# One of four sets of a group's first dense product by seven block products, in a fused attention and MLP kernel

## The chip, the cores and the metric

The kernel runs on one core of a Trainium2 chip. The metric is the device time of one execution in microseconds. The engines are TensorE (PE, with PEld for weight loads), VectorE (DVE), ScalarE (ACT), GpSimd (POOL) and SyncE (SP), which here issues nearly all DMA.

## The reference

Four batches, eight heads, 768 positions, head size 64. For each head, attention with decay `lam` runs over blocks of 64 positions with a carried state; its result is a matrix `x` of 3072 tokens by 512 features. Then comes a dense layer pair:

```
intra = (qb @ kb.T * Dmask) @ vb
inter = (qb * lam_pow) @ kv_state
kv_state = lam**64 * kv_state + (kb * rev_pow).T @ vb
x = (intra + inter), heads side by side          # 3072 x 512
h = x @ w_in                                     # 512 -> 2048
g = gelu_tanh(h)
out = g @ w_out                                  # 2048 -> 512
```

q, k, v and the output are float32; the products inside are in float16 with float32 accumulation.

## The kernel before, in words

**Attention.** There are 24 steps: 12 blocks of 256 tokens, each in two halves of four heads. For a step `s`:

- `load_step` brings q, k and v of the step into pools of four buffers each (`q32`, `k32`, `v32`).
- `cast_qk` (L278, L283) scales q on VectorE and casts k on ScalarE. `scale_v` (L266) scales v on GpSimd. `prep_v` is `scale_v` and the request for the loads of three steps later.
- `transpose_dma` (L293) lays q and k out transposed, by a DMA, in the pool `qkp`. `prep_qk` is `cast_qk` and `transpose_dma`.
- `burst(ns, ss)` does a pair of steps at once: scores S of the steps `ns` (L340), products O of the probabilities of the steps `ss` with v (L424), products K of k and v of the steps `ns` (L438), products of the state u with q of the steps `ss` (L449). VectorE masks the scores into PT (L350) and updates the state t (L491, L494), GpSimd writes u from t (L501), and ScalarE takes the attention result out of PSUM into `xT` (L475).

**The dense layers.** The 12 blocks form seven groups, `[[0, 1], [2], [3], [4, 5], [6, 7], [8, 9], [10, 11]]`, numbered from 0; a group of two blocks has 512 tokens. When a group's `xT` is complete, `queue_group` puts the pieces of its dense products into a list, `filler`. `fill(n)` runs the next n pieces. The calls of `fill` between the parts of the attention are written by hand, so that TensorE has dense work while VectorE, ScalarE and GpSimd prepare the next step.

- First product, plain: `mm1` (L542) makes 128 rows of h for 512 tokens by four products of 128 x 512, and ScalarE's gelu (L546) writes them into `gT`. A group of two blocks has 16 such pieces.
- First product, by seven: for groups in `SEVEN = (5, 6)` (the sixth and seventh) h is cut into four sets. In a set, the blocks of h (two halves of f by two halves of the tokens, contracted over two halves of c) are made from seven block products instead of eight, after Winograd's form of Strassen's scheme. `seven(m, k)` (L711) is product m of set k: four products of 128 x 256. Sums of `w_in` (`sum_win`, L151) and of `xT` (`sum_x`, L690) are the operands. Intermediate results are added outside of TensorE: copies by ScalarE and VectorE (L722, L724), additions by VectorE (L732). PSUM banks HX, HW and HY are opened by products 1, 2 and 5. HX takes products 1, 6, 7 and 4 in turn, and each next product waits until the result so far has been copied or added.
- Second product by seven for the groups from the second on: `product` (L619) with `sum_g` (L589) on VectorE.

[...] a new tile takes a bank whose last reader is done. The order on each engine is the order in which the program is written.

**Around the change.** The fifth group (number 4: blocks 6 and 7, steps 12 to 15) is queued when step 15 is done, in `R(17, 15)`, near 105 us. Its first product runs from 112.65 us, before, between and after the bursts of the steps 18 and 19, and 20 and 21. VectorE makes the last sums of `w_in` (`sum_win(3, ...)`, `sum_win(4, ...)`) just before, since the sixth group needs them.

The lines that bear on it:

```
SEVEN = (5, 6)
...
for i in range(HF):
    for fs in ([[i, i + HF]] if per == 2 else [[i], [i + HF]]):
        filler.append(lambda fs=fs: mm1(fs))
...
            if k == HF // 2 - 1 and m in (3, 7, 4):
                release()
```

`release` issues the gelus that are held back in `pending`; in a set other than the last they wait for product 5 of the next set.

Of the kernel before, what the change touches and what calls it, by code (L numbers as in the profile page):

```python
# [8 lines left out]
FP32 = mybir.dt.float32  # L9
# [6 lines left out]
def kernel(  # L16
# [12 lines left out]
    P = 128  # L29
# [12 lines left out]
    const = ctx.enter_context(tc.tile_pool(name="const", bufs=1))  # L42
# [1 line left out]
    wst = ctx.enter_context(tc.tile_pool(name="wst", bufs=1))  # L44
    ld = ctx.enter_context(tc.tile_pool(name="ld", bufs=4))
    a16p = ctx.enter_context(tc.tile_pool(name="a16", bufs=5))
    qkp = ctx.enter_context(tc.tile_pool(name="qkp", bufs=4))
    ptp = ctx.enter_context(tc.tile_pool(name="ptp", bufs=3))
    ucp = ctx.enter_context(tc.tile_pool(name="ucp", bufs=3))
    ubp = ctx.enter_context(tc.tile_pool(name="ubp", bufs=4))  # L50
# [3 lines left out]
    otp = ctx.enter_context(tc.tile_pool(name="otp", bufs=3))  # L54
# [23 lines left out]
    HF, HE = NF // 2, DM // 2  # L78
# [91 lines left out]
    def load_ahead(s):  # L170
        if s < NSTEP:
            load_step(s)
# [13 lines left out]
                   allow_small_or_imprecise_dtypes=True)  # L186
    nc.gpsimd.tensor_scalar(pos[64:128], pos[64:128], 128.0, None, ALU.subtract)

    rel = const.tile([P, 2, 2, 64], FP32)
    nc.gpsimd.iota(rel[:], pattern=[[-1, 2], [1, 2], [2, 64]], base=0, channel_multiplier=-2,  # L190
                   allow_small_or_imprecise_dtypes=True)
    ident = const.tile([P, P], FP16)
# [30 lines left out]
    def odd(hs):  # L223
        pin(nc.vector.tensor_tensor(dq[:, hs, 1], dq[:, hs, 0], lam_bc[:, hs], ALU.mult))

    def inverse(hs):
        pin(nc.vector.reciprocal(dv[:, hs], dq[:, hs]))
# [21 lines left out]
    def wide(t):  # L249
        return t.rearrange("p j h d -> p h j d")  # L250

    def decay(t, s):
        hs = halves[s % 2]
        return t[:, hs, :].unsqueeze(3).to_broadcast([P, HH, 2, D])

    def prep_v(s):
        scale_v(s)
        if s >= 6:
            if s + 3 == FIRST_DMA_T + 1:
                load_step(s + 3, "qk")  # L260
            else:
                load_ahead(s + 3)

    def scale_v(s):
        tv = a16p.tile([P, 2, HH, D], FP16, tag="v16", name=f"v16_{s}")
        pin(nc.gpsimd.tensor_tensor(wide(tv[:]), ld32[s][2][:], decay(dv, s), ALU.mult))  # L266
        a16[s] = a16[s] + (tv,)

    def prep_qk(s):
        cast_qk(s)  # L270
        transpose_dma(s)

    def cast_qk(s):
        q32, k32, _ = ld32[s]
        tqk = a16p.tile([P, 2, 2, HH, D], FP16, tag="qk16", name=f"qk16_{s}")
        tq, tk = tqk[:, 0], tqk[:, 1]
        q_eng = nc.gpsimd if s == 3 else nc.vector
        pin(q_eng.tensor_tensor(wide(tq), q32[:], decay(dq, s), ALU.mult))  # L278
        if s == 0:
            inverse(halves[0])  # L280
            odd(halves[1])
            inverse(halves[1])
        pin(nc.scalar.activation(out=wide(tk), in_=k32[:], func=AF.Copy))  # L283
        a16[s] = (tq, tk)
        whole_qk[s] = tqk
# [3 lines left out]
    def transpose_dma(s):  # L289
        tqk = whole_qk.pop(s)  # L290
        if s >= FIRST_DMA_T:
            o = qkp.tile([P, 2, 2, 2, P], FP16, tag="qkT", name=f"qkT_{s}")
            pin(nc.sync.dma_start_transpose(out=o[:].rearrange("p a j h t -> p (a j h) t"),  # L293
                                            in_=tqk[:].rearrange("p a j h d -> p (a j h d)")))
            qkT[s] = o
            if s == FIRST_DMA_T:
                load_step(s + 1, "v")
# [219 lines left out]
        return gs_kept[1:]  # L517

    SEVEN = (5, 6)
    SLOTS = {5: {1: 0, 2: 1, 5: 1, 6: 1, 3: 1, 7: 1}, 4: {1: 0, 2: 1, 5: 0, 6: 1, 3: 1, 7: 1}}  # L520
    groups = [[0, 1], [2], [3], [4, 5], [6, 7], [8, 9], [10, 11]]
    group_of = {sb: (g, i) for g, sbs in enumerate(groups) for i, sb in enumerate(sbs)}
    filler = []

    def queue_group(g, lead=0, per_set=0):
# [168 lines left out]
        def release():  # L694
            while pending:
                pending.pop(0)()

        def seven(m, k):

            st = of_set.setdefault(k, {})  # L700
            for name in {1: "X", 2: "W", 5: "Y"}.get(m, ""):
                key = name + str(k % 2) if name == "X" else name
                if key not in hbank:
                    hbank[key] = ps_M.tile([P, 2, SB], FP32, tag="M", name="H" + name)
                st[name] = hbank[key]
            dst = st[{2: "W", 5: "Y", 3: "Y"}.get(m, "X")]
            a, b = X_FACTORS[m]
            for i in range(2):
                f = 2 * k + i
                for c in range(2):  # L710
                    pin(nc.tensor.matmul(  # L711
                        dst[:, i, :],
                        w_in_block(a, slice(c, c + 1), slice(f * P, f * P + P))[:, 0],
                        x_block(b, slice(c, c + 1))[:, 0],
                        start=(m in (1, 2, 5) and c == 0 and i == 0), stop=(m in (2, 3, 4) and c == 1),
                        skip_group_check=True))

            def copied(name, tag, eng):
                t = ld.tile([P, HH, 2, D], FP32, tag=tag, name=f"{name}_{g}_{k}")
                t = t[:].rearrange("p h j d -> p (h j d)").rearrange("p (i t) -> p i t", i=2)  # L720
                if eng is nc.scalar:
                    pin(nc.scalar.activation(out=t, in_=dst[:], func=AF.Copy))  # L722
                else:
                    pin(eng.tensor_copy(out=t, in_=dst[:]))  # L724
                st[name] = t

            def gelu(F, T, src):
                pin(nc.scalar.activation(out=gT[:, 2 * k : 2 * k + 2, F, T * SB : T * SB + SB],
                                         in_=src, func=AF.Gelu_apprx_tanh))

            def added(F, T, name):
                pin(nc.vector.tensor_tensor(st[name], dst[:], st[name], ALU.add))  # L732
                pending.append(lambda src=st[name]: gelu(F, T, src))

            if m == 1:
                copied("m1", "q32", nc.scalar)
            elif m == 2:
                added(0, 0, "m1")
            elif m == 5:
                copied("q", "q32", nc.scalar)  # L740
                release()
            elif m == 6:
                copied("u2", "k32", nc.vector)
            elif m == 3:
                added(0, 1, "u2")
            elif m == 7:
                added(1, 1, "q")
            elif m == 4:
                pending.insert(0, lambda: gelu(1, 0, dst[:]))
            if k == HF // 2 - 1 and m in (3, 7, 4):  # L750
                release()

        def merge(lead, per_set):
# [22 lines left out]
            unread = {1: 16, 2: 12, 4: 8, 3: 4}  # L776
            slots = SLOTS[per_set]
            for k in range(HF // 2):
# [46 lines left out]
        def behind(k, i0, i1, ms):  # L825

            piece = filler[at + k]

            def both():
                piece()  # L830
                sum_g(i0, i1, ms)

            filler[at + k] = both

        at = len(filler)
        order = [(m, p) for m in (1, 2, 5, 6, 3, 7, 4) for p in range(HN // P)]
        if g in SEVEN:
            merge(lead, per_set)
            parts = (0, 1) if g + 1 in SEVEN else (None,)
            for m, p in order:  # L840
# [3 lines left out]
            for k, m in enumerate((2, 4, 3)):  # L844
                behind(len(parts) * k, 4, 8, (m,))
            return
        for i in range(HF):
            for fs in ([[i, i + HF]] if per == 2 else [[i], [i + HF]]):
                filler.append(lambda fs=fs: mm1(fs))
        for m, p in order:  # L850
            for part in (0, 1) if g + 1 in SEVEN else (None,):
                filler.append(lambda m=m, p=p, part=part: product(m, p, part))

        n1 = HF * (2 // per)
        if per == 2:
            behind(5, 0, 4, (1, 2))
            behind(6, 0, 4, (4, 3))
            behind(7, 4, 8, (1,))
            behind(8, 4, 8, (2,))
            behind(9, 4, 8, (4,))  # L860
            behind(10, 4, 8, (3,))
        else:
            behind(9, 0, 4, (1, 2) if g == 3 else (1, 2, 4, 3))
            if g == 3:
                behind(12, 0, 4, (4, 3))
            w = 2 if g + 1 in SEVEN else 1
            for k, m in zip((0, 3, 7, 11) if w == 2 else (0, 1, 2, 4), (1, 2, 4, 3)):
                behind(n1 + k, 4, 8, (m,))

    def fill(n):  # L870
        for _ in range(min(n, len(filler))):
            filler.pop(0)()
# [17 lines left out]
    def U(n):  # L890
        update(n, 1)
# [118 lines left out]
        if n > 8:  # L1010
            sum_win((n - 7) // 2, (n - 1) % 2, nc.vector)

    cast_qk(16)
    scale_v(16)
    fill(3)
    burst((13, 14), (12,))
    transpose_dma(16)
    fill(1)
    U(13)
    U(14)  # L1020
    load_ahead(18)
    load_ahead(19)
    fill(2)
    cast_qk(17)
    scale_v(17)
    fill(3)
    burst((15, 16), (13, 14))
    transpose_dma(17)
    load_ahead(20)
    fill(1)  # L1030
    U(15)
# [12 lines left out]
    sum_win(4, 0, nc.vector)  # L1044
    fill(2)
    sum_win(4, 1, nc.vector)
    fill(2)
    prep_qk(20)
    fill(1)
    prep_qk(21)  # L1050
    prep_v(20)
    fill(3)

    burst((18, 19), (16, 17))
    prep_v(21)
    fill(2)
    U(18)
    U(19)
    fill(4)
    prep_qk(22)  # L1060
    fill(2)
    burst((20, 21), (18, 19), 11, 4)
# [43 lines left out]
```

## Time and profile before

| what | value |
|---|---|
| median of 3 runs | 199.54 us (199.5 to 199.82) |
| span of the profiled execution | 197.7 us |
| TensorE busy | 191.4 us, 97% |
| VectorE, ScalarE, GpSimd busy | 154.0, 122.8, 75.1 us |
| TensorE clock granted | 1.0 over the whole span |
| plain first product of the fifth group | 20 products from 112.81, 32 from 118.95, 12 from 127.49 us |

The span is counted from the first to the last instruction of the profiled execution; the median time is some 1.8 us above it. The page gives for each group of instructions the line, engine and operation, the tiles written and read, count, busy time and mean duration, and the idle time of the engine before it with what ended it.

### The profile page before, as it was taken

How to read it: one execution, taken by the hardware profiler on the slowest of the kernel's cores; microseconds unless marked ns; L12 is line 12 of the kernel's file. 1: busy time of each engine (PE TensorE's matmuls, PEld its weight loads, DVE VectorE, ACT ScalarE, POOL GpSimd, SP SyncE). 2: the span in 40 equal slices, each digit the busy share in tenths (PEclk: the TensorE clock that was granted, in tenths of full speed). 3: DMA queues.
4: the chain of work that ended last, by engine and by line, in shares of the span. 5: the costliest groups of instructions: out<-in, count | busy, mean ns of one | idle time of the engine just before them, and what ended most of it. 6: DMA issues, size and time to landing. Idle time of an engine off the chain costs nothing.

```text
span 197.7 us, 5935 instructions
## 1 busy us (share of the span) xinstructions
PE 191.4 (97%) x2439; PEld 139.8 (71%) x2439; DVE 154.0 (78%) x296; ACT 122.8 (62%) x251; POOL 75.1 (38%) x85
## 2 busy tenths in 40 slices
PE   8879999999999999999999999999999999999993
PEld 2546544456888888754588854578888888888882
DVE  4987722789999989969999927998778996588620
ACT  3673878467794675677645377854768836778221
POOL 6594223456557652455563526156002030002000
PEclk9999999999999999999999999999999999999999
DMA  6999999999999999999993998620211200030205
GB/s 168 290 324 386 386 385 389 297 285 310 335 259 265 218 308 226 195 274 179 286 221 74 235 326 101 174 56 0 53 59 51 106 9 0 0 109 1 106 4 212
DMA packets 61722, 37.86 MB, mean 192 GB/s; under 512 B 17536, under 2 KB 54656, under 8 KB 61696
## 3 DMA queue, kind: packets, MB, share of 16 engines
q1 hardware_dynamic: 61152, 37.23, 74.1%
q8 instruction: 19, 0.31, 0.7%
q10 hardware_dynamic: 544, 0.26, 0.5%
q14 instruction: 7, 0.06, 0.1%
HBM read 27.26 MB, written 6.29 MB: 170 GB/s over the span
## 4 chain that ended last, share of the span: by engine, by line
PE 88%; SPq 4%; DMA 4%; ACT 1%; issue 1%
PE Hps L542 24%; PE MX L619 17%; PE MY L619 9%; PE HX L711 7%; PE O2ps L557 7%; PE MW L619 4%; DMA wi<-in_moe_w_in_dram 4%; SPq L70 4%; PE HY L711 4%; PE S L340 3%; PE Hps L802 3%; PE HW L711 2%; PE OK L398 2%; PE O L449 1%; PE O L424 1%; PE Tps L311 1%
## 5 line engine op out<-in xcount | busy, mean ns | idle before, releaser
L542 PE MATMUL Hps<-xT,w_in 128*128 128x512 f16 (+1 forms) x288 | 50.8, 332 | 0.0
L501 POOL TENSOR_TENSOR u<-t,lumask 128x256 f16<-128x256 f32 x40 | 31.0, 790 | 46.2 <-DVE t L494 28.3
L542 PEld LDWEIGHTS <-w_in 128*128 128x128 f16 x288 | 27.8, 98 | 19.1
L546 ACT ACTIVATE gT<-Hps 128x512 f16<-128x512 f32 x56 | 33.1, 598 | 9.3 <-PE Hps L542 8.8
L350 DVE TENSOR_TENSOR PT<-S,mask 128x512 f16<-128x512 f32 x48 | 30.3, 681 | 6.3 <-PE S L340 6.3
L619 PEld LDWEIGHTS <-gs 128*128 128x128 f16 x320 | 31.2, 98 | 3.6
L266 POOL TENSOR_TENSOR v<-v,dv 128x512 f16<-128x512 f32 x24 | 29.6, 1236 | 8.0 <-DMA v<-in_v_dram 7.7
L619 PEld LDWEIGHTS <-gT 128*128 128x128 f16 x240 | 23.2, 98 | 3.6 <-ACT gT L546 0.5
L619 PE MATMUL MX<-w_sum,gs 128*128 128x256 f16 x160 | 21.4, 273 | 0.0
L278 DVE TENSOR_TENSOR qk<-q,dq 128x512 f16<-128x512 f32 x23 | 19.8, 863 | 0.7 <-DMA q<-in_q_dram 0.7
L664 POOL TENSOR_TENSOR o<-u,q 128x512 f32<-128x512 f32 (+1 forms) x5 | 5.8, 1159 | 37.7 <-ACT u L636 37.7
L283 ACT ACTIVATE qk<-k 128x512 f16<-128x512 f32 x24 | 15.0, 625 | 6.6 <-DMA k<-in_k_dram 6.5
L589 DVE TENSOR_TENSOR gs<-gT 128x1024 f16<-128x1024 f16 (+1 forms) x24 | 17.6, 737 | 1.5 <-ACT gT L546 1.5
L557 PE MATMUL O2ps<-w_out,gT 128*128 128x512 f16 x64 | 14.6, 379 | 0.0
L475 ACT ACTIVATE xT<-OK 128x256 f16<-128x256 f32 x26 | 10.0, 455 | 7.3 <-PE OK L398 7.2
L711 PEld LDWEIGHTS <-ws 128*128 128x128 f16 x128 | 12.5, 97 | 1.8
L636 ACT ACTIVATE u<-MX 128x256 f32<-128x256 f32 x18 | 6.9, 384 | 10.2 <-PE MX L619 10.2
L475 ACT ACTIVATE xT<-O 128x256 f16<-128x256 f32 x22 | 8.0, 460 | 5.9 <-PE O L449 5.0
L557 PEld LDWEIGHTS <-gT 128*128 128x128 f16 x64 | 6.1, 98 | 6.6
L619 PE MATMUL MY<-w_out,gs 128*128 128x256 f16 x80 | 10.7, 273 | 0.0
L340 PEld LDWEIGHTS <-qkT 64*64 64x64 f16 x384 | 6.0, 106 | 6.5 <-issue 3.0
L589 DVE TENSOR_TENSOR gs<-gs,gT 128x1024 f16<-128x1024 f16 (+1 forms) x12 | 10.2, 852 | 0.3
(95 smaller groups left out, 318.7 us busy)
## 6 DMA issues: line engine op xcount, KB each, us to landing
q<-in_q_dram SPq DMA_DIRECT2D x24, 256.0 KB, 5.0
k<-in_k_dram SPq DMA_DIRECT2D x24, 256.0 KB, 5.3
v<-in_v_dram SPq DMA_DIRECT2D x23, 256.0 KB, 5.4
out_dram<-o SPq DMA_DIRECT2D x19, 256.0 KB, 4.0
wo<-in_moe_w_out_dram SPq DMA_DIRECT2D x4, 1024.0 KB, 9.5
wi<-in_moe_w_in_dram SPq DMA_DIRECT2D x4, 512.0 KB, 8.1
wi<-in_moe_w_in_dram SPq DMA_DIRECT2D x2, 1024.0 KB, 12.8
out_dram<-o SPq DMA_DIRECT2D x2, 512.0 KB, 6.8
```

The lines of the kernel that those rows point to most:

```text
L266: pin(nc.gpsimd.tensor_tensor(wide(tv[:]), ld32[s][2][:], decay(dv, s), ALU.mult))
L278: pin(q_eng.tensor_tensor(wide(tq), q32[:], decay(dq, s), ALU.mult))
L283: pin(nc.scalar.activation(out=wide(tk), in_=k32[:], func=AF.Copy))
L350: pin(nc.vector.tensor_tensor(t[:, hl].rearrange("p b c d -> p b (c d)"), Sps[:].rearrange("p b c d -> p b (c d)"), mask[:].unsqueeze(1).t ...
L475: pin(nc.scalar.activation(out=d, in_=o, func=AF.Copy))
L501: pin(nc.gpsimd.tensor_tensor(u[:], state[half][:].unsqueeze(2).to_broadcast([P, 2, 2, D]), lumask[:, 2 * half : 2 * half + 2, :].unsqueez ...
L542: pin(nc.tensor.matmul(by_block(Hps[:, i, :]), w_in16[:, c, f * P : (f + 1) * P], x(c), start=(c == 0), stop=(c == NC - 1)))
L546: pin(nc.scalar.activation(out=dst, in_=Hps[:], func=AF.Gelu_apprx_tanh))
L557: pin(nc.tensor.matmul(O2[tau][0][:], gT[:, f % HF, f // HF, tau * P : (tau + 1) * P], w_out16[:, f, :], start=(n == 0), stop=(n == NF - 1)))
L589: pin(nc.vector.tensor_tensor(g_rows(m, i), g_rows(a, i), g_rows(b, i), op))
L619: pin(nc.tensor.matmul(dst, lhsT, rhs, start=(opens and i == 0), stop=(closes and i == HF - 1), skip_group_check=True))
L711: pin(nc.tensor.matmul(dst[:, i, :], w_in_block(a, slice(c, c + 1), slice(f * P, f * P + P))[:, 0], x_block(b, slice(c, c + 1))[:, 0], sta ...
```

## The change

One of the four sets of the fifth group's first product (f = 0, 1, 8, 9) is made by seven block products; the other twelve pieces stay plain. The pieces of the set are queued alternating with three of the plain ones, and the gelus are issued as soon as their operands are there. The sums of `w_in` exist already at that time, the sums of `xT` (`sum_xs[0](m)`) are called by hand. To go with it, the pool `qkp` gets a fifth buffer, and `rel`, which is needed only at the start, takes a buffer of the pool of outputs to make space. Transposes of steps 16 and 17 are issued with their casts, and the hand-written order around the bursts of steps 18 to 21 moves: all the seven products of the set come ahead of the burst of 18 and 19, and v of steps 20 and 21 is scaled later.

```diff
-    qkp = ctx.enter_context(tc.tile_pool(name="qkp", bufs=4))
+    qkp = ctx.enter_context(tc.tile_pool(name="qkp", bufs=5))
...
-    rel = const.tile([P, 2, 2, 64], FP32)
+    rel = otp.tile([P, 2, 2, 64], FP32, tag="o32", name="rel")
...
+    MIXED = 4
+    sum_xs = []
...
-            if k == HF // 2 - 1 and m in (3, 7, 4):
+            if (k == HF // 2 - 1 or g == MIXED) and m in (3, 7, 4):
                 release()
...
-        for i in range(HF):
+        if g == MIXED:
+            sum_xs.append(sum_x)
+            plain = [[f] for i in range(2, HF) for f in (i, i + HF)]
+            for m in (1, 2, 5, 0, 6, 3, 0, 7, 0, 4):
+                filler.append((lambda m=m: seven(m, 0)) if m else (lambda fs=plain.pop(0): mm1(fs)))
+            for fs in plain:
+                filler.append(lambda fs=fs: mm1(fs))
+        for i in range(HF) if g != MIXED else ():
...
-            behind(9, 0, 4, (1, 2) if g == 3 else (1, 2, 4, 3))
+            n1 += 3 * (g == MIXED)
+            behind(n1 - 7, 0, 4, (1, 2) if g == 3 else (1, 2, 4, 3))
...
-    cast_qk(16)
+    prep_qk(16)
     scale_v(16)
     fill(3)
     burst((13, 14), (12,))
-    transpose_dma(16)
     fill(1)
...
-    cast_qk(17)
+    prep_qk(17)
     scale_v(17)
     fill(3)
     burst((15, 16), (13, 14))
-    transpose_dma(17)
     load_ahead(20)
...
     sum_win(4, 1, nc.vector)
-    fill(2)
+    for m in (1, 2, 3, 4):
+        sum_xs[0](m)
     prep_qk(20)
-    fill(1)
+    fill(3)
     prep_qk(21)
+    fill(8)
+
+    burst((18, 19), (16, 17))
     prep_v(20)
-    fill(3)
-
-    burst((18, 19), (16, 17))
-    prep_v(21)
     fill(2)
     U(18)
     U(19)
-    fill(4)
+    prep_v(21)
+    fill(2)
     prep_qk(22)
     fill(2)
     burst((20, 21), (18, 19), 11, 4)
```

## The prediction

> **What bounds the kernel now.** I read the page's busy times and slices first, then the chain of waits, then the table of stretches around the change, then the timelines of VectorE and GpSimd there.
>
> ```profile
> PE 191.4 (97%) x2439; PEld 139.8 (71%) x2439; DVE 154.0 (78%) x296; ACT 122.8 (62%) x251; POOL 75.1 (38%) x85
> PE   8879999999999999999999999999999999999993
> ...
> 112.81 4.32 PE Hps L542 x20
> 117.13 0.57 PE S L340 x32
> 117.70 0.45 PE O L424 x32
> 118.15 0.25 PE K L438 x32
> 118.40 0.55 PE O L449 x8
> 118.95 6.91 PE Hps L542 x32
> 125.86 0.57 PE S L340 x32
> 126.43 0.45 PE O L424 x32
> 126.88 0.28 PE K L438 x32
> 127.16 0.33 PE O L449 x4
> 127.49 2.59 PE Hps L542 x12
> ```
>
> From about 20 us on TensorE never stops: the list of what TensorE waited for holds 3.1 us in all, none of it after 95 us, and the chain through the changed stretch is TensorE from piece to piece. So a microsecond of products taken away is a microsecond gained, and any new wait of TensorE is paid in full. The question is whether the other engines can follow.
>
> ```profile
> 120.28 1.18 POOL L501 TENSOR_TENSOR u<-t,lumask 128x256 f16<-128x256 f32 x2 [5.46 <-DVE t L491]
> 121.42 1.04 POOL L266 TENSOR_TENSOR v<-v,dv 128x512 f16<-128x512 f32 x1
> 122.42 2.08 POOL L501 TENSOR_TENSOR u<-t,lumask 128x256 f16<-128x256 f32 x2
> ...
> 122.21 0.81 DVE L589 TENSOR_TENSOR gs<-gT 128x1024 f16<-128x1024 f16 x1 [1.04 <-ACT gT L546]
> 123.05 0.98 DVE L589 TENSOR_TENSOR gs<-gs,gT 128x1024 f16<-128x1024 f16 x1
> 124.07 0.98 DVE L589 TENSOR_TENSOR gs<-gT,gs 128x1024 f16<-128x1024 f16 x1
> 124.98 0.68 DVE L589 TENSOR_TENSOR gs<-gT 128x1024 f16<-128x1024 f16 x1
> 125.58 0.68 DVE L278 TENSOR_TENSOR qk<-q,dq 128x512 f16<-128x512 f32 x1
> 126.25 0.69 DVE L350 TENSOR_TENSOR PT<-S,mask 128x512 f16<-128x512 f32 x1
> ```
>
> These lines carry the forecast. Two u products take 1.18 us while VectorE works from PSUM, and 2.08 us beside the sums gs; the sums take 0.98 beside u and 0.68 once GpSimd is done. The two engines take turns here. Taken apart, a blocked u needs 0.47 us when its turn comes (124.50 - 124.03) and a blocked sum 0.55 (125.05 - 124.50). The v product needs 1.04 free (121.42) and 0.90 after being blocked: at 113.33 it waits for qk, which ends at 113.92, and ends itself at 114.82. VectorE reaches the first PT of step 20 at 126.25, with the scores that feed it at 125.79: no slack.
>
> [...] 3.49/32 = 0.109 us, 4.32/20 = 0.216. [...]
>
> **The change part by part.**
>
> 1. Products. Sixteen 512-column products (f 0, 1, 8, 9) go: 16 x 0.216 = 3.46 us. Seven times four of 256 columns come: 28 x 0.109 = 3.06. On TensorE, so **-0.40**. Where before 20 wide products (4.32) stood ahead of the burst of scores 18 and 19, there are now 28 narrow and 12 wide (5.65): that burst moves 1.33 later. After it 24 wide replace 32 (5.18 for 6.91), so the burst of 20 and 21 comes 0.40 earlier if nothing waits.
>
> 2. Five buffers; transposes of 16, 17 and 20 no longer held back; rel in the pool of outputs. The fifth buffer lets transpose 20 go about 4 us earlier. No row of TensorE waits on a transpose here (21 was issued at 120.2 and landed within 4.7 us, before 125.8), so 0. Transpose 21 still waits for a buffer of the burst; it is issued near 120.6 and lands by 125.3, before its score in every case. The other moves of 16 and 17 keep the order of the DMA queue: 0.
>
> 3. Inside the seven products. VectorE is the late one: before, it finished the weight sums at 111.64. Now come four sums of x, the q cast of 20, an addition, the q cast of 21, a copy and two additions. The GpSimd addition at 111.56 takes its 1.13 turn (before, from the end of cast 20 at 112.24 to 113.37) after the first sum, to 113.11; sums of x cost 0.41, 0.28 once blocked, then 0.33 apart (starts 130.83 and 131.16): to 114.06. Everything else starts 0.60 apart: cast 20 to 114.66, added m1 115.26, cast 21 115.86, u2 116.46, u3 117.06. ScalarE's copy of the fifth product needs the q buffer that cast 20 frees, so it ends at 115.38, where TensorE wanted that bank at 112.65 + 2.61 = 115.26. The addition into q ends near 118.03; TensorE wants its bank at 118.01. About **+0.2** together; 0 to 0.5.
>
> 4. HX is held until the last gelu. In the order of the two builds, the K1 bank of burst (18, 19) is now the bank of HX, freed only by gelu(1,0). ScalarE runs gelu of q, gelu of the third plain pair and gelu of HX after 118.07, 0.55 to 0.6 apart: HX free at 119.9. TensorE wants K1 0.92 after its scores begin at 118.6, at 119.5: **+0.4** (0 if ScalarE is not behind, 0.6 at most). K, O and the first wide product then start at 120.75, where it was 118.79.
>
> 5. prep_v(20) goes behind the burst, prep_v(21) behind U(18), U(19). GpSimd's order was v20 early, then u18, u19, v21, u18, u19; now it is u18, u19, v20, u18, u19, v21, all after the burst. Burst (20, 21) multiplies K of step 21 by v21 before the rest of the burst and all queued products. PT of step 18 starts 0.46 after its scores: 119.06; four PT and the first t end at 121.74; u's end at 123.0. The sums gs start when the first wide product behind the burst has its gelu (ScalarE is past its four xT copies at about 122.2): 122.7. Turns: gs to 123.4, v20 124.3, gs 124.85, u 125.3, gs 125.9, u 126.35, gs 126.9, v21 127.8, cast 22 to 128.35. TensorE starts scores 20 at 120.75 + 5.18 + 0.09 = 126.02 and K21 0.92 + 0.175 later: 127.1. It waits until 127.85: **+0.7**. With no blocking at all v21 would end at 126.7 and the wait would be 0; with cast 22 ahead of v21 it is 1.3.
>
> 6. PT of step 20 stands behind cast 22, so its first half ends at 128.35 + 0.6 = 128.95. The first wide product after the burst takes the bank it reads, and would start 127.85 + 0.44 = 128.3: **+0.7** (0 if cast 22 went first, since then item 5 has it).
>
> 7. 1.3 us more of ScalarE (two copies at 0.6, gelus 0.03 longer) fits its 6.4 busy in 10 us, but for item 4. The sums gs of group 4 hang behind piece 12 where it was 9, with two banks' rows done earlier: counted in item 5.
>
> Sum: -0.40 + 0.2 + 0.4 + 0.7 + 0.7 = +1.6. After that TensorE has nothing to give it back with: it is full to the end. 199.54 + 1.6 = **201.1 us**.
>
> **The rivals.**
>
> Saving kept. GpSimd and VectorE clash less than I count, v21 is there in time, and the waits of 3 and 4 hide in rounding: 199.54 - 0.40 = 199.15. For it: moving v20 away leaves VectorE undisturbed from 113.1 to 118, which is where item 3 needs it. [...] 13 in 100.
>
> Saving eaten by the seven products alone. Waits 3 and 4 cost 0.2 + 0.4, v21 is just in time: 199.75. Against: v21 has two u, one v and four sums more ahead of it than the 4.2 us from 123 to 127.1 can hold. 10 in 100.
>
> One of items 5 and 6 alone. v21 ends at 127.3 to 127.5 and PT waits little: 199.75 + 0.3 to 0.7, so 200.3. 17 in 100.
>
> DMA becomes the bound: q, k, v of step 23 are asked for later and 21's transpose lands behind other loads. The share of DMA falls to 0.37 by 128 to 132 us, and step 23 is read after 135: in no case over 0.1, and within the others.
>
> **How the numbers follow.** Forecast 60, one of 5 and 6 alone 17, no change 10, saving kept 13. Slower 0.77, same 0.10, faster 0.13. Item 5 at its high end with 3 and 4 at theirs gives 201.9. The low end takes in the no-change case and most of its spread, 199.3.
>
> **What would show it.** Right: TensorE waits on GpSimd's v (K, L438) near 127 us, a wait on ScalarE's gelu of HX at the K of the burst before, a wait on PT at the first wide product after 128, and a span about 1.6 longer with 28 narrow products taking 3.06 us. Wrong: no wait of TensorE on v, with v21 ending before K21 asks. If the products waited on VectorE inside the seven for over 0.5 us, item 3 was the mis-sized term.

## The result and the profile after

The changed kernel takes 202.37 us (median of 5 runs, 202.13 to 202.76) where the kernel before takes 199.54 (199.4 to 199.82): ratio 1.0137, 95% interval 1.0117 to 1.0156. That is slower, by 2.8 us where 1.6 were forecast, and above the range, which ended at 201.9. The profiled executions differ by as much: spans of 200.6 and 197.7 us.

First the page of the changed kernel, busy times and slices:

```profile
PE 192.7 (96%) x2451; PEld 141.9 (71%) x2451; DVE 158.1 (79%) x304; ACT 123.9 (62%) x253; POOL 74.6 (37%) x85
...
PE   8979999999999999999999999799999999999992
```

Behind the start, one slice shows a hole: the 26th, 125.4 to 130.4 us, stands at 7. What TensorE waited for in the whole execution names it (engine, tile and line, what released it: us in total, times, longest):

```profile
PE K L438 <- POOL v L266: 0.7, 1, 0.7
...
PE Hps L544 <- DVE PT L350: 0.5, 1, 0.5
PE S L340 <- DMA qkT<-qk: 0.3, 1, 0.3
PE K L438 <- ACT gT L730: 0.3, 1, 0.3
```

These four are new. Three are those of items 4, 5 and 6; the transposed q and k of step 16 (DMA qkT) are not. The timeline of TensorE after the change shows where they stand, and its starts give their true size (a wait in brackets is counted from the modelled end of a matmul, and comes out smaller than the gap between starts):

```profile
115.30 0.60 PE L713 MATMUL HX<-xs,ws 128*128 128x256 f16 x4
115.73 0.60 PE L713 MATMUL HY<-xT,ws 128*128 128x256 f16 x4
...
118.94 0.64 PE L340 MATMUL S<-qkT 64*64 64x128 f16 x32
...
119.86 0.19 PE L438 MATMUL K<-v,qk 64*64 64x64 f16 x1
120.30 0.44 PE L438 MATMUL K<-v,qk 64*64 64x64 f16 x31 [0.25 <-ACT gT L730]
...
126.41 0.64 PE L340 MATMUL S<-qkT 64*64 64x128 f16 x32
...
127.33 0.29 PE L438 MATMUL K<-v,qk 64*64 64x64 f16 x16
128.33 0.32 PE L438 MATMUL K<-v,qk 64*64 64x64 f16 x16 [0.71 <-POOL v L266]
...
129.48 1.89 PE L544 MATMUL Hps<-xT,w_in 128*128 128x512 f16 x8 [0.50 <-DVE PT L350]
```

From 41 us up to the scores of step 16 the starts in the two traces agree within 0.04 us. Starts of the same piece from there on, and what each step of the shift is:

| piece on TensorE | before | after | shift | the step |
|---|---|---|---|---|
| O products behind the scores of step 16 | 94.80 | 95.28 | +0.48 | wait for the transpose of step 16 |
| scores of 18 and 19 | 117.06 | 118.94 | +1.88 | narrow products come first (+1.33); +0.07 for the waits inside the seven |
| u products of burst (18, 19) | 118.33 | 120.68 | +2.35 | K1 waits for the gelu of HX: +0.47 |
| scores of 20 and 21 | 125.79 | 126.41 | +0.62 | 1.33 given back, and the 0.40 saved |
| u products of burst (20, 21) | 127.09 | 128.59 | +1.50 | K21 waits for v21: +0.88 |
| first wide product behind them | 127.32 | 129.48 | +2.16 | waits for PT of step 20: +0.66 |
| start of the last product | 194.29 | 196.45 | +2.16 | nothing won or lost |
| end of the span | 197.7 | 200.6 | +2.9 | another 0.75, behind the start of the last product |

So 2.2 us arise on TensorE and 0.75 us behind its last product. The cause of the 0.75 shows in the view of DMA at the end, from just before the last store is issued to the end of the span (40 slices; the digits are the busy share, below them GB/s). Before:

```profile
GB/s 29 263 410 410 439 380 351 380 410 380 234 59 0 102 249 366 351 351 307 132 15 0 0 0 0 0 0 0 0 0 0 0 0 0 0 0 0 0 0 0
...
q1 hardware_dynamic: 288, 0.39, 39.0%
```

After:

```profile
GB/s 0 182 387 387 364 387 364 455 296 92 0 159 319 432 319 194 34 0 0 0 0 23 34 23 11 0 0 0 0 0 0 0 0 0 0 0 0 0 0 0
...
q1 hardware_dynamic: 288, 0.39, 30.2%
q14 instruction: 1, 0.01, 1.2%
```

The same 288 packets, but the last few come alone, at 11 to 34 GB/s, after a gap. A packet of another queue lies in this window, by the queue's name a fetch of instructions (q14), from 198.19 to 198.90 us; the kernel before has none of these between 161.75 and 198.22, when its last store had landed (at 196.36) and its span had ended. In the changed kernel the last nine packets of the store start one after the other from 198.90 on, the moment at which the fetch ends. From the issue of the last store to its last packet it is 1.36 us before and 2.08 after.

### The profile page after: what moved, and what is told of

Read it like the earlier page. It is cut to its first block, busy times and chain, and to the rows that moved or that the text cites. A ratio compares the mean times of both kernels' runs of the same rounds, so it can differ in the third digit from the quotient of the medians.

```text
span 200.6 us, 5972 instructions
## 1 busy us (share of the span) xinstructions
PE 192.7 (96%) x2451; PEld 141.9 (71%) x2451; DVE 158.1 (79%) x304; ACT 123.9 (62%) x253; POOL 74.6 (37%) x85
## 4 chain that ended last, share of the span: by engine, by line
PE 71%; DVE 9%; DMA 8%; SPq 4%; ACT 3%; issue 1%; DVEq 0%
PE Hps L544 16%; PE MX L621 14%; PE HX L713 7%; PE MY L621 7%; PE O2ps L559 7%; DMA wi<-in_moe_w_in_dram 4%; SPq L70 4%; PE HY L713 4%; PE MW L621 3%; PE Hps L804 3%; DMA qkT<-qk 3%; PE S L340 2%; DVE gs L591 2%; DVE qk L278 2%; PE HW L713 2%; DMA q<-in_q_dram 2%
## 5 line engine op out<-in xcount | busy, mean ns | idle before, releaser
L544 PE MATMUL Hps<-xT,w_in 128*128 128x512 f16 (+1 forms) x272 | 47.7, 329 | 0.5 <-DVE PT L350 0.5
L544 PEld LDWEIGHTS <-w_in 128*128 128x128 f16 x272 | 26.2, 98 | 17.4 <-issue 0.6
L548 ACT ACTIVATE gT<-Hps 128x512 f16<-128x512 f32 x52 | 30.7, 597 | 8.7 <-PE Hps L544 8.2
L621 PEld LDWEIGHTS <-gT 128*128 128x128 f16 x240 | 23.2, 98 | 3.6 <-ACT gT L548 0.5
L278 DVE TENSOR_TENSOR qk<-q,dq 128x512 f16<-128x512 f32 x23 | 18.7, 814 | 0.6 <-DMA q<-in_q_dram 0.5
L713 PEld LDWEIGHTS <-ws 128*128 128x128 f16 x144 | 14.1, 98 | 2.4
L713 PEld LDWEIGHTS <-w_in 128*128 128x128 f16 x108 | 10.6, 98 | 1.7 <-issue 0.2
L591 DVE TENSOR_TENSOR gs<-gs,gT 128x1024 f16<-128x1024 f16 (+1 forms) x12 | 11.1, 923 | 0.3
L713 PE MATMUL HX<-xs,ws 128*128 128x256 f16 x72 | 10.8, 273 | 0.0
```

Source lines behind the costliest of these rows:

```text
L544: pin(nc.tensor.matmul(by_block(Hps[:, i, :]), w_in16[:, c, f * P : (f + 1) * P], x(c), start=(c == 0), stop=(c == NC - 1)))
L548: pin(nc.scalar.activation(out=dst, in_=Hps[:], func=AF.Gelu_apprx_tanh))
L591: pin(nc.vector.tensor_tensor(g_rows(m, i), g_rows(a, i), g_rows(b, i), op))
L621: pin(nc.tensor.matmul(dst, lhsT, rhs, start=(opens and i == 0), stop=(closes and i == HF - 1), skip_group_check=True))
L713: pin(nc.tensor.matmul(dst[:, i, :], w_in_block(a, slice(c, c + 1), slice(f * P, f * P + P))[:, 0], x_block(b, slice(c, c + 1))[:, 0], sta ...
```

## The experiments

The theory: on TensorE the waits of items 4 to 6 are one chain. VectorE is late inside the seven products, and behind the burst GpSimd and VectorE take turns (in the changed kernel v takes 1.49 us and the sum gs beside it 1.41; before the change a sum with GpSimd idle takes 0.68), so that removing one wait brings another. The 0.75 at the end belongs to a fetch of instructions that the few more instructions of ScalarE put beside the last store; the 0.48 at step 16 is an accident of the DMA queue. The rivals: the waits are independent and can be removed one by one; VectorE is too full wherever v stands; the end is lengthened by the store itself; the wait at step 16 comes from the five buffers and the moved transposes. Ratios are to the kernel before, run on the same chip; the chip differs between some of the experiments, so they are compared by their ratios.

**e1, v scaled earlier, in the changed kernel.** Step 20's v goes ahead of the burst, 21's directly behind it.

```diff
     prep_qk(21)
+    scale_v(20)
     fill(8)
     burst((18, 19), (16, 17))
-    prep_v(20)
+    load_ahead(23)
+    prep_v(21)
     fill(2)
     U(18)
     U(19)
-    prep_v(21)
```

> The changed kernel, but v of step 20 is scaled ahead of the burst of 18 and 19 and v of step 21 right after it, ahead of U(18) and U(19), as before; the loads of step 23 stay after the burst. Theory [...]: the wait of K21 on v (0.9 us between the products in the changed kernel) and that of the first wide product on PT (0.66) go; v20 again takes its turn of 0.9 us among VectorE's work for the seven products and gives back 0.2 to 0.6 there. 201.0 us, 200.8 to 201.4, against 202.37. Rival (VectorE is simply 5 us fuller with its eight additional instructions, wherever v stands): the first wide product after the burst of 20 and 21 still waits on PT, and at most 0.5 us is won: 201.9 or more.

202.26 us against 199.77, ratio 1.0111 (1.0079 to 1.0143). The wait for v21 is gone, that for PT is not, and in the waits of TensorE a new one stands ahead of them:

```profile
PE HY L713 <- ACT q L724: 0.7, 1, 0.7
...
PE Hps L544 <- DVE PT L350: 0.5, 1, 0.5
...
PE K L438 <- ACT gT L730: 0.3, 1, 0.3
```

GpSimd's v20, 1.22 us from 113.57, now runs beside VectorE's sums of x:

```profile
113.81 1.26 DVE L692 TENSOR_TENSOR xs<-xT 128x512 f16<-128x512 f16 x1
...
115.33 0.68 DVE L278 TENSOR_TENSOR qk<-q,dq 128x512 f16<-128x512 f32 x1
```

This third sum takes 0.41 us in the changed kernel, and cast 20 starts there at 114.31 (0.18 of the difference are an earlier shift). The copy of q hangs on this cast, and product 3 starts 0.83 us late. The time and the wait for PT are as the recorded rival had them, and the recorded theory, that both waits go, failed: earlier is no remedy. Removing a wait brought another, as in the theory above, but whether VectorE is too full wherever v stands is left to e8.

**e2, only v late, in the kernel before.**

```diff
-    prep_v(20)
     fill(3)
     burst((18, 19), (16, 17))
-    prep_v(21)
+    prep_v(20)
     fill(2)
     U(18)
     U(19)
+    prep_v(21)
```

> The kernel before, with v of the steps 20 and 21 scaled as late as in the changed kernel, and nothing else. Theory: the order of GpSimd by itself costs: v21 is there just in time, at about 126.1, for K21 at 126.9, but cast 22 and PT of step 20 follow later, and the first wide product waits 0.5 for PT: 200.0 us, 199.8 to 200.6. Rival (the move is harmless by itself and the seven products' 1.3 us later burst is what makes v late): 199.5, within 0.2.

200.05 us against 199.77, ratio 1.0015 (0.9993 to 1.0037): the interval holds 1, so the time decides nothing. The profile has the wait of the first wide product for PT (0.44 by starts), none for v21. Without the seven products v21 is there in time, so the late v alone makes only a part of item 6. In the waits of this execution step 16 waits for its transpose too (0.38 by starts), though nothing before step 20 is changed:

```profile
PE Hps L542 <- DVE PT L350: 0.3, 1, 0.3
...
PE S L340 <- DMA qkT<-qk: 0.2, 1, 0.2
```

**e3, only the buffers and the transposes, in the kernel before.**

```diff
-    qkp = ctx.enter_context(tc.tile_pool(name="qkp", bufs=4))
+    qkp = ctx.enter_context(tc.tile_pool(name="qkp", bufs=5))
...
-    rel = const.tile([P, 2, 2, 64], FP32)
+    rel = otp.tile([P, 2, 2, 64], FP32, tag="o32", name="rel")
...
-    cast_qk(16)
+    prep_qk(16)
...
-    transpose_dma(16)
```

and the same for 17.

> The kernel before with five buffers of transposed queries and keys, rel in the pool of outputs, and the transposes of 16 and 17 issued with their casts; no seven products, no move of v. Theory A (these edits make the transpose of step 16 late): TensorE waits about 0.5 us at the scores of step 16, 200.0 us. Theory B (that wait of the changed kernel is the accident of a DMA queue that ran 0.9 us late from about 55 us on): no wait there or a wait that differs in size, 199.5 within 0.2.

199.63 us against 199.77, ratio 0.9989 (0.9973 to 1.0006). Most of its 21 runs lie between 199.5 and 199.75; the profiled one is the slowest, 201.31, and its waits show why:

```profile
PE S L340 <- DMA qkT<-qk: 1.1, 1, 1.1
```

By starts it is 1.26 us. So the wait at step 16 is not a fixed cost of these edits: to judge by their times most runs don't have it, and a kernel without them can have it (e2). Each kernel has one trace; of the 14 traces seven show this wait, from 0.22 to 1.26 us, two of the five from kernels without the seven products and five of the nine from kernels with them. How many of the five runs of the changed kernel contain it isn't known.

**e4 and e6, eight and three tiny copies on ScalarE, in the kernel before.** They are placed at the start, where constants are made, and move only the number of ScalarE's instructions.

```diff
+    spare = const.tile([P, 8], FP16)
+    for i in range(8):
+        pin(nc.scalar.activation(out=spare[:, i : i + 1], in_=ident[:, i : i + 1], func=AF.Copy))
```

> The kernel before with eight copies of 128 x 1 on ScalarE at the start, where it waits for the first load; their results are not used. Theory (the changed kernel's last store is 0.75 us longer because the additional instructions of ScalarE make a fetch of instructions fall beside the last store): the end moves by 0.75, 200.3 us. Rival (the fetch belongs to VectorE, or has nothing to do with it): 199.5, within 0.2, with no fetch of instructions between the last product and the end.

Eight: 199.68 us against 199.77, ratio 0.9994 (0.9978 to 1.001). The expected loss did not come. The trace shows the fetch not beside the store but well ahead of it, at 193.01 us, 9 us before the end. (This profiled execution had a clock of 0.95, so only the place of the fetch is read from it.) The changed kernel has three more recorded instructions of ScalarE (322 against 319, of which the page counts 253 and 251), so three was tried next:

> The kernel before with three unused copies of 128 x 1 on ScalarE, as many instructions more as ScalarE has in the changed kernel. Theory: the fetch of instructions comes beside the last store and the end is 0.5 to 0.75 us later: 200.0 to 200.5 where the kernel before on the same chip has 199.6 to 199.8. Rival: no difference, within 0.2.

Three: 200.43 us against 199.63, ratio 1.0032 (1.0015 to 1.0049), as expected. The view of DMA around its last store has the same picture as the changed kernel, a fetch, a gap and a trickle:

```profile
GB/s 298 372 372 348 397 348 397 372 149 0 74 273 410 323 348 137 25 0 0 12 25 25 25 12 0 0 0 0 0 0 0 0 0 0 0 0 0 0 0 0
...
q14 instruction: 1, 0.01, 1.1%
```

From the start of the last product to the end of the span it takes 3.95 us here, 3.38 in the kernel before, 4.14 in the changed one. Here too the last nine packets of the store begin when the fetch ends, at 196.83.

**e5, the eight copies in the changed kernel.** The edit is that of e4.

> The changed kernel with eight unused copies of 128 x 1 on ScalarE at the start. The fetches in the records say that a fetch of instructions belongs to ScalarE: with three instructions more it came beside the last store, with eight more in the kernel before it came 9 us before the end. Theory: here it comes some 7 us before the end, the last store is as short as before, and 0.75 us is won: 201.6, 201.4 to 201.9. Rival (the long end of the changed kernel is the store's own): 202.4, within 0.3.

201.6 us against 199.63, ratio 1.009 (1.0055 to 1.0126). The fetch is at 185.24 us, 15 us before the end where the author's estimate was 7, and the end takes 3.37 us again: 0.76 back there, by instructions that do nothing. With four runs the interval of the ratio overlaps that of the changed kernel, so the times alone would not show it; e9, with the same eight copies, has 201.57. The later experiments build on this version, so that the end doesn't blur them.

**e7, one copy moved from VectorE to ScalarE (on e5).**

```diff
-                copied("u2", "k32", nc.vector)
+                copied("u2", "k32", nc.scalar if g == MIXED else nc.vector)
```

> The changed kernel with the eight unused copies, and with the copy u2 of the mixed set on ScalarE instead of VectorE: 0.6 us less for VectorE ahead of the burst, 0.6 more for ScalarE. Theory A (VectorE has too much between 108 and 129 us, and every 0.6 us shows): the waits on v and PT shrink by 0.3 to 0.6, 201.1 to 201.3. Theory B (only GpSimd's order and ScalarE's gelu of HX count; VectorE waits for the burst's scores in any case, 1.0 us at 118.4): nothing is won, and the wait at K of the burst before grows: 201.6 to 202.0.

202.52 us against 199.63, ratio 1.0128 (1.0092 to 1.0165), above the ranges of both theories and no better than e5, though four runs from 201.82 to 203.12 can't rank the two. All three waits stay (0.6 for v21, 0.5 for PT, 0.3 for K1), and one of 0.26 before product 7 joins them, since on ScalarE the copy stands behind two gelus (117.92, where product 7 could have had the bank at 118.30 and gets it at 118.56). Taking 0.6 us from VectorE shortened nothing; as theory B had it, VectorE waits there in any case, in the changed kernel 1.04 us for the scores of the burst (PT at 119.40).

**e8, v where VectorE works from PSUM (on e5).** A copy of one column, which reads the result of cast 21, holds GpSimd back until VectorE is past the sums of x; v20 follows. Step 21's v stands inside the burst, ahead of u.

```diff
+    pin(nc.gpsimd.tensor_copy(out=warm[:], in_=a16[21][0][:, 0, 0, 0:1]))
+    scale_v(20)
     fill(8)
-    burst((18, 19), (16, 17))
-    prep_v(20)
+    burst((18, 19), (16, 17), mid=lambda: scale_v(21))
+    load_ahead(23)
     fill(2)
     U(18)
     U(19)
-    prep_v(21)
```

> The changed kernel with the eight unused copies; v of step 20 is scaled after cast 21 (a copy of one column of that cast on GpSimd holds it back until then), while VectorE works from PSUM, and v of step 21 in the burst of 18 and 19 ahead of the first u. Theory [...]: no wait of K21 on v, VectorE's sums are blocked by two u alone, PT wait at most 0.4: 200.3, 200.0 to 200.7. Rival (VectorE by itself is too full, as in the run with v back in its old place, where the waits came back elsewhere): 201.2 or more.

200.21 us against 199.63, ratio 1.003 (1.0015 to 1.0045). Two waits are gone, as the theory had it; that for HX (0.47) and 0.15 inside the seven are left. In the timeline of GpSimd both v take 1.04 us, where the changed kernel has 1.49 beside VectorE's sums of gelus. Here VectorE copies and adds from PSUM during the first (`u<-HX` from 115.81, `u<-HY` from 116.62) and masks the scores during the second (PT from 119.08):

```profile
116.09 1.04 POOL L269 TENSOR_TENSOR v<-v,dv 128x512 f16<-128x512 f32 x1
119.58 1.04 POOL L269 TENSOR_TENSOR v<-v,dv 128x512 f16<-128x512 f32 x1 [2.44 <-PE O L427]
121.84 3.22 POOL L506 TENSOR_TENSOR u<-t,lumask 128x256 f16<-128x256 f32 x4 [1.22 <-DVE t L496]
```

VectorE gains by it too. Two of its sums and cast 22 are shorter:

```profile
123.61 0.98 DVE L596 TENSOR_TENSOR gs<-gs,gT 128x1024 f16<-128x1024 f16 x1
...
125.54 0.68 DVE L596 TENSOR_TENSOR gs<-gT 128x1024 f16<-128x1024 f16 x1
126.14 0.68 DVE L281 TENSOR_TENSOR qk<-q,dq 128x512 f16<-128x512 f32 x1
```

In the changed kernel they take 1.41, 1.10 and 1.52 us, together 1.7 us more.

**e9, gelu of HX first (on e5), and e10, the same on e8.** The gelu of HX goes ahead of the gelu of q.

```diff
-            if (k == HF // 2 - 1 or g == MIXED) and m in (3, 7, 4):
+            if m in (3, 4) and g == MIXED or k == HF // 2 - 1 and m in (3, 7, 4):
```

> The changed kernel with the eight unused copies, and with ScalarE's gelu of HX ahead of the gelu of q (v as in the changed kernel). Theory (HX comes free 0.5 us earlier, so K of the burst of 18 and 19 no longer waits; but v of step 21 and PT of step 20 are set by the turns of GpSimd and VectorE, which do not hang on that wait): the 0.45 us comes back in the wait of K21 on v, and the time stays at 201.6, within 0.2. Rival (waits of TensorE add up one by one): 201.15.

201.57 us against 199.6, ratio 1.0115 (1.0085 to 1.0146): nothing won, as the theory had it. The waits of TensorE have no K for a gelu any more, and v21 costs what that gave:

```profile
PE K L441 <- POOL v L269: 1.2, 1, 1.2
```

(With the eight copies in the file, its line numbers are three higher.)

> The run with v in the free places, and ScalarE's gelu of HX ahead of that of q. Both theories: the wait of 0.47 at K of the burst of 18 and 19 goes. Theory (there PT of step 20 has 0.2 us to spare): at least 0.2 and at most 0.45 us is won over that run, so the median comes to 199.75 to 200.0 where that run has 200.2, and the kernel before 199.6 to 199.7. Rival (PT then waits as long): 200.2.

199.69 us against 199.6, ratio 1.0008 (0.9998 to 1.0019). Where v no longer binds, the same edit brings the ratio from 1.003 to 1.0008: the K1 wait of 0.47 goes, and a part of it comes back as the one wait of the stretch left in the list (0.32 by starts):

```profile
PE Hps L549 <- DVE PT L353: 0.2, 1, 0.2
```

**e11 and e12, the rest (on e10).** e11 puts `prep_qk(20)` ahead of the sums of x; e12 moves one of the four sums of gelus behind the burst of 20 and 21.

```diff
-            behind(n1 - 7, 0, 4, (1, 2) if g == 3 else (1, 2, 4, 3))
+            behind(n1 - 7, 0, 4, (1, 2) if g == 3 else (1, 2, 4))
+            if g == MIXED:
+                behind(n1 + 11, 0, 4, (3,))
```

> As the run before it, and q of step 20 is cast ahead of the sums of x, so that the q buffer for the fifth product's copy is free earlier. Theory: the wait of 0.15 us of the third product on that copy goes, and the sums of x are still in time: 0.1 to 0.15 us less than the run before it. Rival (a sum of x that is not there in time makes the fifth or sixth product wait): the same or up to 0.3 more.

e11: 199.94 us against 199.6, ratio 1.0012 (0.9999 to 1.0024). Nothing is won, as the recorded rival had it. By starts the wait for the copy of q (0.13) is gone, and product 5 waits 0.18 for the sum of x that now comes later.

> Theory: what is left in the version with the gated v and the turned gelus is VectorE's lateness before the PT copy of step 20 (wait 0.17 us at the first wide product) and a q-copy wait of 0.13; moving the first of the three partial sums of group 4's gelus (0.6 us of VectorE) behind the wide products takes the PT wait away: about 0.2 below that version, ratio to the kernel before about 0.9985 to 0.9995, 199.4 to 199.6 us. Rival: VectorE is full in the following stretch too, and the sum comes back as a wait there: ratio 1.000 to 1.002, 199.7 to 200.0 us.

e12: 200.05 us against 199.66, ratio 1.0019 (1.0004 to 1.0033). The wait for PT is gone, as the theory had it, and another of about its size comes 10 us later: in its timeline of TensorE, HX of the next group starts 0.73 us after the four products ahead of it, where four such products take 0.44:

```profile
138.91 0.60 PE L626 MATMUL MX<-w_sum,gs 128*128 128x256 f16 x4
139.64 0.60 PE L718 MATMUL HX<-xs,ws 128*128 128x256 f16 x4
```

VectorE's copy that frees this bank starts at 138.90, where e10 has it at 137.45; 0.97 of these 1.45 us are the shift of the whole stretch (the first wide product, 128.37 against 127.40), the rest comes from the moved sum, which VectorE does just ahead of it. The rival's range holds the ratio and the theory's does not: VectorE is full there too.

## Why the prediction was wrong, step by step

The direction and the three waits were right, each with the cause that the prediction gave it. By its items:

- Item 1 (-0.40, the burst 1.33 later and 0.40 earlier): right. The shift falls by 1.73 = 1.33 + 0.40 from the one burst to the other. The 0.109 us for 256 columns is read from the chain before, 32 such products in 3.49 us:

```profile
109.32 3.49 PE MX L619 x32
```

- Item 2 (0): no cost of these edits shows in e3. But "No row of TensorE waits on a transpose here" was read from one execution; in that of the changed kernel step 16 waits 0.48 for its transpose. Part of the difference between the two profiled spans is such chance.
- Item 3 (+0.2, 0 to 0.5): +0.07 measured. HY starts at 115.73, with nothing lost that can be told from rounding. Other executions of the same order lose more there: in the trace of e5 product 3 waits 0.36 for the copy of q.
- Item 4 (+0.4): +0.47, with the gelu of HX from 119.66.
- Item 5 (+0.7): +0.88. The turns came exactly as listed: gs, v20, gs, u, gs, u, gs, v21, cast 22, each about 0.5 us later than listed, which is the wait of step 16. The timelines of GpSimd and of VectorE in the changed kernel have the two late v, and the sums and the cast that take up to 1.41 and 1.52 us where the kernel before has 0.68 to 0.98 and 0.68:

```profile
123.31 1.49 POOL L266 TENSOR_TENSOR v<-v,dv 128x512 f16<-128x512 f32 x1
124.76 2.08 POOL L501 TENSOR_TENSOR u<-t,lumask 128x256 f16<-128x256 f32 x2
126.80 1.49 POOL L266 TENSOR_TENSOR v<-v,dv 128x512 f16<-128x512 f32 x1
...
123.08 0.81 DVE L591 TENSOR_TENSOR gs<-gT 128x1024 f16<-128x1024 f16 x1
123.93 1.41 DVE L591 TENSOR_TENSOR gs<-gs,gT 128x1024 f16<-128x1024 f16 x1
125.38 0.98 DVE L591 TENSOR_TENSOR gs<-gT,gs 128x1024 f16<-128x1024 f16 x1
126.28 1.10 DVE L591 TENSOR_TENSOR gs<-gT 128x1024 f16<-128x1024 f16 x1
127.31 1.52 DVE L278 TENSOR_TENSOR qk<-q,dq 128x512 f16<-128x512 f32 x1
128.75 2.47 DVE L350 TENSOR_TENSOR PT<-S,mask 128x512 f16<-128x512 f32 x4
```

- Item 6 (+0.7): +0.66. PT of step 20 starts at 128.75, where 128.35 was forecast.
- Items 1 and 3 to 6 together: +1.7, against +1.6. That the sum is so near is in part luck: item 3 came out 0.13 below its term and item 5 0.18 above.
- **The step that failed** is the sum and, ahead of it, item 7: "After that TensorE has nothing to give it back with: it is full to the end. 199.54 + 1.6". TensorE gave nothing back, but the sum takes what comes behind its last product as unchanged, a term put at nothing without a reason. Item 7 priced ScalarE's added work as busy time alone. Its three added instructions also moved a fetch of instructions beside the last store, +0.75. e5 takes this away at the end of the span without touching the work, e6 brings it about in the kernel before. With it and the 0.48 of step 16 the sum is 1.7 + 0.75 + 0.48 = 2.9, which is the difference of the spans. The high end of the range doesn't come out of its terms either: items 3 to 5 at theirs, with item 6 then at 0 as it says itself, give 199.54 - 0.40 + 0.5 + 0.6 + 1.3 = 201.5 and not 201.9.

What stays open: of e5 only one execution is profiled, its slowest (202.53). It reaches step 16 0.82 us late, most of it a wait for a gelu near 60 us, and waits 0.22 there. Its median of 201.6 is 2.0 above the kernel before, where the measured items give 1.7; how the rest of 0.3 divides isn't shown. Nor is it settled whether the changed order makes the wait at step 16 likelier: e3 speaks against a fixed cost of the moved transposes, and seven waits in 14 traces are too few to tell. What makes the transpose late is open too.

Of the rivals, "saving kept" has its limit shown by e10: with v, the gelus and the fetch all put right the kernel is level with the one before, not 0.4 faster. In the trace of e10 the 0.40 is saved, and 0.20 in the seven products and 0.32 before the first wide product take it back. Both waits are for VectorE or for what it frees, and the table of stretches shows why. Its columns are the stretch and its length, then busy us (instructions) of TensorE, weight loads, VectorE, ScalarE and GpSimd. Before:

```profile
112.00:117.00 5.00, 5.00 (x28) 2.44 (x25) 1.92 (x2) 3.93 (x8) 2.82 (x2) 1.00 1.17 278
117.00:125.80 8.80, 8.80 (x140) 4.73 (x140) 7.17 (x15) 6.41 (x13) 4.22 (x5) 1.00 0.90 187
125.80:131.00 5.20, 5.20 (x123) 3.63 (x123) 5.09 (x12) 3.79 (x9) 1.37 (x2) 1.00 0.45 97
```

After:

```profile
112.00:118.90 6.90, 6.90 (x52) 4.81 (x50) 6.13 (x10) 5.30 (x11) 1.39 (x1) 1.00 1.33 235
118.90:126.40 7.50, 7.25 (x130) 4.00 (x128) 6.90 (x14) 5.97 (x13) 4.24 (x5) 1.00 0.76 186
126.40:131.00 4.60, 3.38 (x109) 2.29 (x109) 4.60 (x6) 2.58 (x6) 1.88 (x2) 1.00 0.50 104
```

VectorE goes from 14.2 to 17.6 busy us of the same 19, and in the last stretch it has no idle time at all while TensorE stands at 3.38 of 4.60. The 0.40 us of TensorE cost 3.4 busy us of VectorE; the 1.7 us by which two sums and cast 22 take longer than in e8 are part of it. VectorE had been idle for 3.1 of 5.0 us in the first stretch, but for 0.1 of 5.2 in the last. Over the same 19 us of e10, with TensorE's waits nearly gone, VectorE is busy for 17.6 as well.

## What to carry to other kernels

Before products are taken from a full TensorE, look whether the engines that do the additions are free from there until the next slack, not just beside the products: here VectorE was idle for 3.1 of 5.0 us in one stretch, but for 1.6 of 8.8 and 0.1 of 5.2 in the next two, and waits removed one at a time (e1, e9) came back elsewhere. Where GpSimd and VectorE take turns, try GpSimd's work beside VectorE's work from PSUM (with that order v took 1.04 us in e8 instead of 1.49, and two waits went). Compare the time behind the last product too, and look for instruction fetches there, before a small loss or gain is put down to the change itself.

## What the runs showed of the hardware

- v on GpSimd took 1.04 us beside VectorE's copies, additions and masks from PSUM (e8) and 1.49 beside its sums gs and cast 22 (the changed kernel). A sum gs took 0.68 us with GpSimd idle, 0.98 beside u (the kernel before) and 1.41 beside v and u (the changed kernel). What makes the two engines lengthen each other's work no trace shows.
- With a fetch of instructions (q14) beside the last store, the end took 3.93 to 4.14 us from the start of the last product, in three of the 14 traces (the changed kernel, e1, e6); in the others, e4 left out, it took 3.37 to 3.57. In all three the last nine packets of the store begin within 0.01 us of the end of the fetch (198.90, 198.92, 196.83); that they stood behind it is read from that, and wasn't tried apart.
- The fetch moved when ScalarE alone got more instructions; no trace names the engine that it serves. With three more than in the kernel before it fell beside the store (e6: 3.95 us for the end, against 3.38). With eight more it came at 193.01 us, 9 us before the end (e4, ratio 0.9994), and with eight more than in the changed kernel at 185.24, 15 us before the end (e5, 3.37 us for the end).
- TensorE's wait for the transpose of step 16 was between 0 and 1.26 us in the 14 traces, and no edit goes with it. The programs of e5 and e7 to e12 are the same up to there; they waited 0.22, 1.07, 0, 0, 0, 0 and 1.09.
